# Routing one block's attention logits through DRAM, and retiming a selector group and the last staged stores, in a four-layer transformer kernel

## The chip, the cores and the metric

The kernel runs on one core of a Trainium2 chip. The metric is device time in microseconds (us). A core has a tensor engine (PE, with its weight loads PEld), a vector engine (DVE), a scalar engine (ACT), a general one (POOL) and a sync engine (SP). SP's in-order queue issues nearly all DMAs here.

## The reference

Input x is 2048 tokens of 1024 bf16 numbers. Two kinds of layer alternate, twice each, every one behind a layer norm and with a residual addition:

- Attention: x @ wqkv, 32 heads of 32. Token s looks at tokens s, s-2, ..., s-14 (8 of them). The logits are 8 dot products of length 32 per head and token; then softmax, weighted values, and @ wo.
- Gated feed-forward: relu(x @ W_gate) * (x @ W_up), 3584 wide, then @ W_down.

```
idx = pos[:, None] - arange(8) * 2
logits = einsum("bhsd,bhswd->bhsw", q, k[idx]) * 32 ** -0.5     # masked where idx < 0
o = einsum("bhsw,bhswd->bhsd", softmax(logits), v[idx]) @ wo
x = x + o;   h = relu(x @ W_gate) * (x @ W_up);   x = x + h @ W_down
```

## The kernel before

Tokens are worked in blocks of 512; a layer pair has 4 blocks, and the two pairs make blocks 0 to 7. PE does the projections and the feed-forward; DVE does the attention proper. While PE is in block n's feed-forward, DVE works on block n+1's attention. The whole program is a list of events with planned times; sorting it fixes the order on each engine. Orders are not changed at run time: a late item holds up what stands behind it in its engine's queue.

A matmul of 512 columns is a unit of 0.216 us; a group of 8 (one accumulator, "a chunk") takes GRP = 1.73 us. `acc` tiles rotate through 6 accumulators.

The logits: DVE multiplies q and k and sums over 8 chunks into s (128 partitions x 8 offsets x 512 tokens). Each head's sum is still spread over 4 partitions. It is finished in one of two ways:

```
def head_mm(n):                 # blocks 0 and 1: a "selector group" of 8 short matmuls on PE, into tile L
    for wh in range(2):         # two halves: offsets 0 to 3, then 4 to 7
        for tq in range(TPB):
            mm(st["L"][32*tq:32*tq+32, WH*wh:WH*(wh+1), :], lhsT=sel[:],
               rhs=st["s"][:, WH*wh:WH*(wh+1), tq*P:(tq+1)*P], ...)

def store_s(n): sp_dma(s_d[n % 2][:], att[n]["s"][:]...)   # other blocks: 1 MB to DRAM,
def load_s(n):  ...   # read back in 4 DMAs of 256 KB so that a head's 4 partial sums lie on one partition,
def head_sum(n):      # and added on DVE:
    dv(nc.vector.tensor_tensor, u[:], s4[:, 0:2], s4[:, 2:4], op=ALU.add)
    dv(nc.vector.tensor_tensor, u[:, 0], u[:, 0], u[:, 1], op=ALU.add)

def shift(): Lt = st["L"][:] if n < 2 else head_sum(n)
```

In the first 190 us q and k of blocks 1 to 3 go to DRAM through a pool of 6 staging tiles (`qst`, `kst`). When the first feed-forward starts, that memory is handed to its hidden tiles (r, hT), so the first relu waits for the last staged store to land:

```
pool["stage"] = ...                        # 6 staging tiles
ev.append((t_gu0 - 0.01, start_hidden))    # closes "stage", opens "hid"
spread(puts[ahead:], t_fill + GRP + 1.2, GRP)         # the last staged stores; the very last at t_gu0 + 1.2
# weight slabs (1 MB each, a ring of 5): the next one is issued 0.3 us after the end of an old slab's use
events.append((ends[i - RING] + 0.3 if i >= RING else 0.1 * i, f))
```

`[cut: layer norms, projections, weighted values (pv), output store and load (o_d, oT), output projection (wo), down projection]`

## Time and profile before

| | before |
|---|---|
| time, median of 4 runs | 1623.07 us (1621.28 to 1624.59); 1623.55 of 3 when the prediction was made |
| profiled span | 1620.6 us |
| PE busy, and its share of the chain that ended last | 99%, 93% |
| DVE busy | 70%, dense only from 40 to 370 us |
| first value matmul / last matmul starts | 9.99 / 1617.33 us |

The page's engine line (busy us, share, instructions) and its chain line (shares of the chain that ended last):

```profile
PE 1609.6 (99%) x7513; PEld 784.4 (48%) x7562; DVE 1135.1 (70%) x961; ACT 475.8 (29%) x971; POOL 174.1 (11%) x164
PE 93%; DVE 4%; DMA 1%; issue 1%; ACT 0%; SPq 0%; DVEq 0%; POOL 0%; ACTq 0%
```

99% busy does not say how much can be won. The Trainium skill ("Perfetto Trace Analysis", Identifying the Most-Contended Engine) warns that matmul busy share is a poor measure of headroom because matmuls are pipelined, and advises (Optimization Strategy) looking for the gaps on the bottleneck engine and for what ended them. This trace agrees that the share hides losses: a group of 8 is shown as 1.89 us long, but the next one starts 1.73 us after it, so a lost 0.16 us doesn't show as idle. (The page says that pipelined instructions look smaller in a trace; here they look longer, 379 ns each at starts 216 ns apart. The profiler models their ends.) The thing to read is the time from one start to the next, 0.216 us when nothing is lost. Apart from the first 10 us, PE departs from that in only three places (a distance of exactly two pitches is a matmul whose record is missing from the trace, and is passed over).

From the view of waits (engine, line, tile <- releaser: us in total, times, longest):

```profile
PE L L132 <- DVE s L106: 2.0, 2, 1.1
PE acc_g L132 <- ACT r L730: 0.2, 1, 0.2
ACT r L730 <- DMA k_d<-kst: 9.2, 1, 9.2
```

Place 1, the selector group of block 0, in the timeline (start us, duration us, engine, line, what, count, [idle before <- what ended it]):

```profile
99.17 0.40 PE L132 MATMUL L<-s,sel 128*32 128x512 bf16 x4
100.41 0.40 PE L132 MATMUL L<-s,sel 128*32 128x512 bf16 x4 [0.84 <-DVE s L106]
100.74 22.62 PE L132 MATMUL acc_v<-xnT_a,w_v 128*128 128x512 bf16 x104
```

The matmul before it started at 98.86 (99.17 less 0.31). It is 1.88 us to the next ordinary one, in place of 0.216: the second half waits for DVE to finish the second half of s. Place 2, the same in block 1:

```profile
228.88 1.89 PE L132 MATMUL acc_u<-xnT_b,w_u 128*128 128x512 bf16 x8
230.70 0.40 PE L132 MATMUL L<-s,sel 128*32 128x512 bf16 x4
232.24 0.40 PE L132 MATMUL L<-s,sel 128*32 128x512 bf16 x4 [1.14 <-DVE s L106]
232.57 1.90 PE L132 MATMUL acc_g<-xnT_b,w_g 128*128 128x512 bf16 x8
```

Here it is 2.18 us from the last `acc_u` start (230.39) to the `acc_g` at 232.57. Place 3 begins on SP. Its last k store is issued behind two weight slabs, and ACT's first relu needs that store's landing (the third line from the end is from the chain of waits in order of time: start, us, what):

```profile
191.83 0.39 SPq L121 DMA_DIRECT2D w_u<-in_B_W_up_dram  x1
192.46 0.46 SPq L121 DMA_DIRECT2D w_g<-in_B_W_gate_dram  x1
193.12 2.93 SPq L121 DMA_DIRECT2D k_d<-kst  x1
193.12 9.00 DMA k_d<-kst
202.34 1.57 ACT L730 ACTIVATE r<-acc_g 128x512 bf16<-128x512 f32 x3 [9.25 <-DMA k_d<-kst]
202.99 1.89 PE L132 MATMUL acc_g<-xnT_b,w_g 128*128 128x512 bf16 x8 [0.20 <-ACT r L730]
```

The slabs landed at 198.98 and 201.81 us, the 128 KB store at 202.12. Relu stood still for 9.25 us; PE could fill its six accumulators meanwhile (6 x 1.73 = 10.4 us) and lost only 0.36 us (0.58 between starts instead of 0.22).

### The profile page before, as it was taken

How to read it: one execution, taken by the hardware profiler on the slowest of the kernel's cores; microseconds unless marked ns; L12 is line 12 of the kernel's file. 1: busy time of each engine (PE TensorE's matmuls, PEld its weight loads, DVE VectorE, ACT ScalarE, POOL GpSimd, SP SyncE). 2: the span in 40 equal slices, each digit the busy share in tenths (PEclk: the TensorE clock that was granted, in tenths of full speed). 3: DMA queues.
4: the chain of work that ended last, by engine and by line, in shares of the span. 5: the costliest groups of instructions: out<-in, count | busy, mean ns of one | idle time of the engine just before them, and what ended most of it. 6: DMA issues, size and time to landing. Idle time of an engine off the chain costs nothing.

```text
span 1620.6 us, 18710 instructions
## 1 busy us (share of the span) xinstructions
PE 1609.6 (99%) x7513; PEld 784.4 (48%) x7562; DVE 1135.1 (70%) x961; ACT 475.8 (29%) x971; POOL 174.1 (11%) x164
## 2 busy tenths in 40 slices
PE   9999999999999999999999999999999999999999
PEld 6646544444444445444454444544445444444444
DVE  6999899995979699929479294892939939311211
ACT  4853221042116223613136031360313311131110
POOL 2300100010002002300053000530005100000000
PEclk9999999999999999999999999999999999999999
DMA  9868855689569857794757948479574884655452
GB/s 296 182 191 245 211 175 188 196 198 251 166 195 202 204 181 234 182 231 153 223 176 189 240 156 224 159 205 245 173 227 154 206 246 156 208 162 176 156 166 68
DMA packets 402695, 315.82 MB, mean 195 GB/s; under 512 B 162096, under 2 KB 384688, under 8 KB 400944
## 3 DMA queue, kind: packets, MB, share of 16 engines
q1 hardware_dynamic: 402032, 314.03, 68.4%
q8 instruction: 59, 0.97, 0.3%
q10 hardware_dynamic: 576, 0.59, 0.1%
q14 instruction: 28, 0.23, 0.0%
HBM read 265.24 MB, written 33.61 MB: 184 GB/s over the span
## 4 chain that ended last, share of the span: by engine, by line
PE 93%; DVE 4%; DMA 1%; issue 1%; ACT 0%; SPq 0%; DVEq 0%; POOL 0%; ACTq 0%
PE acc_g L132 23%; PE acc_u L132 23%; PE dacc L132 18%; PE acc_wo L132 7%; PE acc_k L132 6%; PE acc_q L132 6%; PE acc_v L132 6%; PE dacc_pair L132 6%; DVE ac L106 2%; DVE t L106 2%; DMA k_d<-kst 1%; DMA w_v<-in_A_wqkv_dram 0%; DVE s L106 0%; DVE hT L106 0%; ACT xn_a L263 0%
## 5 line engine op out<-in xcount | busy, mean ns | idle before, releaser
L132 PE MATMUL acc_g<-xnT_b,w_g 128*128 128x512 bf16 x1792 | 423.4, 379 | 0.2 <-ACT r L730 0.2
L132 PE MATMUL acc_u<-xnT_b,w_u 128*128 128x512 bf16 x1792 | 423.4, 379 | 0.0
L730 ACT ACTIVATE r<-acc_g 128x512 bf16<-128x512 f32 x224 | 133.4, 596 | 725.4 <-PE acc_g L132 660.5
L106 DVE TENSOR_TENSOR hT<-acc_u,r 128x512 bf16<-128x512 f32 x224 | 151.2, 690 | 238.2 <-PE acc_u L132 234.1
L132 PE MATMUL dacc<-w_d,hT 128*128 128x512 bf16 (+1 forms) x1372 | 300.4, 375 | 1.5
L132 PEld LDWEIGHTS <-hT 128*128 128x128 bf16 x1820 | 178.0, 98 | 209.0
L132 PEld LDWEIGHTS <-w_g 128*128 128x128 bf16 x1792 | 175.3, 98 | 211.7 <-issue 0.7
L132 PEld LDWEIGHTS <-w_u 128*128 128x128 bf16 x1792 | 175.3, 98 | 211.5
L106 DVE TENSOR_TENSOR pv<-a,vhm 128x4096 bf16<-128x4096 bf16 x64 | 143.7, 2290 | 0.0
L549 DVE TENSOR_TENSOR t<-q,k 128x2048 f32<-128x2048 bf16 x56 | 128.1, 2293 | 6.7 <-ACT k L485 4.6
L777 DVE TENSOR_TENSOR x<-dacc,x 128x512 bf16<-128x512 f32 (+1 forms) x38 | 24.5, 673 | 154.1 <-PE dacc L132 154.1
L106 DVE TENSOR_TENSOR t<-q,k 128x2048 f32<-128x2048 bf16 x56 | 127.6, 2289 | 4.0 <-ACT k L485 2.4
L106 DVE TENSOR_TENSOR pv<-pv 128x1024 bf16<-128x1024 bf16 (+1 forms) x128 | 113.9, 956 | 0.0
L132 PE MATMUL acc_wo<-w_o,oT 128*128 128x512 bf16 x498 | 111.1, 379 | 0.7
L562 DVE TENSOR_TENSOR ac<-ac,t 128x2048 f32<-128x2048 f32 x48 | 109.7, 2286 | 0.3
L106 DVE TENSOR_TENSOR ac<-ac,t 128x2048 f32<-128x2048 f32 x48 | 109.8, 2287 | 0.0
L490 POOL COPY kh<-k 128x14 bf16<-128x14 bf16 x40 | 53.7, 1347 | 511.0 <-ACT k L485 511.0
L249 POOL TENSOR_TENSOR st_b<-st_b,neg_half 128x1 f32<-128x1 f32 x29 | 40.2, 1394 | 609.7 <-ACT st_b L248 609.7
L132 PE MATMUL dacc_pair<-w_d,hT 128*128 128x512 bf16 x413 | 95.5, 379 | 0.4
L132 PEld LDWEIGHTS <-oT 128*128 128x128 bf16 x512 | 50.1, 98 | 60.3
L244 ACT ACTIVATE xn_b<-x 128x1024 bf16<-128x1024 bf16 x29 | 30.3, 1045 | 125.0 <-DVE x L703 62.1
L410 ACT CAST vT<-acc_v 128x512 bf16<-128x512 f32 x56 | 32.6, 585 | 54.8 <-PE acc_v L132 54.8
(131 smaller groups left out, 1225.2 us busy)
## 6 DMA issues: line engine op xcount, KB each, us to landing
w_g<-in_B_W_gate_dram SPq DMA_DIRECT2D x56, 1024.0 KB, 6.9
w_u<-in_B_W_up_dram SPq DMA_DIRECT2D x56, 1024.0 KB, 5.2
w_d<-in_B_W_down_dram SPq DMA_DIRECT2D x48, 1024.0 KB, 6.0
w_o<-in_A_wo_dram SPq DMA_DIRECT2D x16, 1024.0 KB, 7.1
vhm<-v_d SPq DMA_DIRECT2D x32, 284.0 KB, 6.8
v_d<-vT SPq DMA_DIRECT2D x8, 1024.0 KB, 9.3
oT<-o_d SPq DMA_DIRECT2D x32, 256.0 KB, 4.1
w_d<-in_B_W_down_dram SPq DMA_DIRECT2D x16, 512.0 KB, 3.8
```

Of the source, the lines that this page charges most:

```text
L106: tail_dve[0] = f(*args, **kwargs).ins
L132: tail_pe[0] = nc.tensor.matmul(*args, **kwargs).ins
L244: nc.scalar.activation(xn, xt[:], ACT.Square, accum_out=sq)
L249: nc.gpsimd.tensor_tensor(rstd, vpe, neg_half[:, 0:1], op=ALU.pow)
L410: tail_act[0] = nc.scalar.copy(st["vT"][:, c, :], acc[:]).ins
L490: nc.gpsimd.tensor_copy(khalo[n][:, c, :], k[:, BLK:BLK + HALO])
L549: nc.vector.tensor_tensor(t[:], i0, i1, op=ALU.mult)
L562: nc.vector.tensor_tensor(o, ac[:], t[:], op=ALU.add)
L730: tail_act[0] = nc.scalar.activation(rs[j][:], acc[:], ACT.Relu).ins
L777: run = dv if n < NB - 2 else (lambda f, *args, **kwargs: f(*args, **kwargs))
```

## The change

Its intent: take block 1's selector group off PE, remove block 0's wait, and get the last staged store ahead of the slabs. For the first of these, block 1's logits go through DRAM as the later blocks' do; the sums are stored by halves, so that the first half is away before the second is computed. Everything behind is given new times. The core of it:

```
-            sp_dma(s_d[n % 2][:], att[n]["s"][:].rearrange("p w t -> p (w t)"))
+            ws = slice(WH * half, WH * (half + 1))
+            sp_dma(s_d[n % 2][:, ws, :], att[n]["s"][:, ws, :])
...
-            Lt = st["L"][:] if n < 2 else head_sum(n)
+            Lt = st["L"][:] if n == 0 else head_sum(n)
...
-    ev.append((t_v2 + 2.2 * GRP, lambda: head_mm(0)))         # block 0's group a chunk later
-    spread(softmax_steps(0), t_v2 + 2.3 * GRP, 0.01)
+    ev.append((t_v2 + 3.2 * GRP, lambda: head_mm(0)))
+    spread(softmax_steps(0), t_v2 + 3.3 * GRP, 0.01)
...
-    spread(puts[ahead:], t_fill + GRP + 1.2, GRP)             # last staged store before the slabs
+    ev.extend((min(t_fill + GRP * (i + 1) + 1.2, t_gu0 + 0.2), f) for i, f in enumerate(puts[ahead:]))
...
-    spread(sums1[4:6], t_wo0 + 1.0, 2.5)
+    spread(sums1[4:6], t_wo0 + 0.5, 2.5)
...
-    t_head1 = t_gu0 + 37.0
-    ev.append((t_head1, lambda: head_mm(1)))
-    spread(softmax_steps(1), t_head1 + 0.1, 3.5)
...
         if n == 0:
-            spread(pv_steps(1), t_head1 + 11.5, 5.5)
-            ev.append((at + 102.0, store_o(1)))
-            ev.append((at + 102.1, load_o(1)))
+            ev.append((at + 4.0, store_s(1, 0)))
+            ev.append((at + 37.5, store_s(1, 1)))
+            ev.append((at + 40.5, load_s(1)))
             spread(gets2, at + 36.0, 2.5)
-            spread(prod_sum_steps(2), t_head1 + 11.5 + 44.5, 5.0)
+            spread(softmax_steps(1), at + 52.0, 3.6)
+            spread(pv_steps(1), at + 63.0, 5.3)
+            ev.append((at + 88.0, store_o(1, 0, 4)))
+            ev.append((at + 106.0, store_o(1, 4, 8)))
+            ev.append((at + 106.1, load_o(1)))
+            spread(prod_sum_steps(2), at + 106.0, 4.9)
...          # blocks 2 and 3: sums and outputs by halves too, times moved a few us; blocks 4 to 7: sums by halves
```

More of the change, by code (lines that the diff above doesn't have):

```diff
@@ L161 @@
     k_d = dram.tile([KC, P, S], BF16, name="k_d")
-    s_d = [dram.tile([P, W * BLK], BF16, name=f"s_d{i}") for i in range(2)]
+    s_d = [dram.tile([P, W, BLK], BF16, name=f"s_d{i}") for i in range(2)]
     zpad = const.tile([P, KC, HALO], BF16, name="zpad")
@@ L564, in prod_sum_steps, with store_s @@
         return [mult(h, c) for h in range(2) for c in range(KC)]
-    def store_s(n):
+    def store_s(n, half):
         def f():
-            sp_dma(s_d[n % 2][:], att[n]["s"][:].rearrange("p w t -> p (w t)"))
+            ws = slice(WH * half, WH * (half + 1))
+            sp_dma(s_d[n % 2][:, ws, :], att[n]["s"][:, ws, :])
         return f
@@ L924 @@
         if n == 0:
-            spread(pv_steps(1), t_head1 + 11.5, 5.5)
-            ev.append((at + 102.0, store_o(1)))
-            ev.append((at + 102.1, load_o(1)))
+            ev.append((at + 4.0, store_s(1, 0)))
+            ev.append((at + 37.5, store_s(1, 1)))
+            ev.append((at + 40.5, load_s(1)))
             spread(gets2, at + 36.0, 2.5)
-            spread(prod_sum_steps(2), t_head1 + 11.5 + 44.5, 5.0)
-        elif n + 1 < NN:
-            t_s = at + (29.0 if n < NB - 1 else 0.4)
-            ev.append((t_s - (6.0 if n < NB - 1 else 3.5), store_s(n + 1)))
-            ev.append((t_s, load_s(n + 1)))
-            spread(softmax_steps(n + 1), t_s + 13.6, 3.6)
-            spread(pv_steps(n + 1), t_s + 24.6, 6.0)
-            ev.append((t_s + 79.6, store_o(n + 1)))
-            ev.append((t_s + 79.7, load_o(n + 1)))
-            if n == 1:
-                spread(gets3, at + 24.0, 2.5)
-                spread(prod_sum_steps(3), t_s + 76.0, 4.9)
+            spread(softmax_steps(1), at + 52.0, 3.6)
[4 more added lines that the diff above has]
+            spread(prod_sum_steps(2), at + 106.0, 4.9)
+        elif n + 1 < NB:
+            ev.append((at - 8.0, store_s(n + 1, 0)))
+            ev.append((at + 28.5, store_s(n + 1, 1)))
+            ev.append((at + 32.0, load_s(n + 1)))
+            if n == 1:
+                spread(gets3, at + 46.0, 2.5)
+                spread(prod_sum_steps(3), at + 103.0, 4.9)
+            spread(softmax_steps(n + 1), at + 45.0, 3.6)
+            spread(pv_steps(n + 1), at + 56.0, 5.5)
+            ev.append((at + 79.0, store_o(n + 1, 0, 4)))
+            ev.append((at + 102.0, store_o(n + 1, 4, 8)))
+            ev.append((at + 102.1, load_o(n + 1)))
+        elif n + 1 < NN:
+            ev.append((at - 3.2, store_s(n + 1, 0)))
+            ev.append((at - 3.1, store_s(n + 1, 1)))
+            ev.append((at + 0.4, load_s(n + 1)))
+            spread(softmax_steps(n + 1), at + 14.0, 3.6)
+            spread(pv_steps(n + 1), at + 25.0, 6.0)
+            ev.append((at + 80.0, store_o(n + 1)))
+            ev.append((at + 80.1, load_o(n + 1)))
         if NB <= n + 2 < NN:
```

## The prediction

> **What bounds it now.** The tensor engine. The page gives PE 1609.6 us of a 1620.6 us span (99%) and PE 93% of the chain that ended last; granted clock 1.0. DVE is 70% busy, dense only from 40 to 370 us. Matmuls of 512 columns start 0.216 us apart. The PE timeline has only three wider gaps after the first 10 us; from 233 us to the last matmul at 1617.3 us there is none. The Trainium skill ("Perfetto Trace Analysis", Identifying the Most-Contended Engine) calls matmul busy share a poor measure, so I use starts. Only these can be won:
> 1. Selector group of block 0: its second half waits 0.84 us for DVE's s. From the value matmul before it to the next (100.74) takes 1.86 us; without a wait about 0.96 (0.31 + 0.33 + 0.32).
> 2. Selector group of block 1: a wait of 1.14 us; 2.16 us from the up matmul before it to the gate matmul after it (232.57).
> 3. At 202.99 PE waits for a gate buffer (0.58 between starts, not 0.22). ACT's relu stood 9.25 us behind the last staged k store, issued at 193.12 and landed at 202.12 behind two 1 MB slabs (issued 191.83 and 192.46, landed 198.98 and 201.81).
>
> **What the change does.**
> - Block 0's group a chunk (1.73 us) later: the wait goes, the group stays: −0.9 us.
> - Block 1 without the group: −1.94 us of PE. DVE pays two additions (2.29 + 1.22 us, as block 2 pays), DMA 1 MB out and back.
> - Last k store ahead of the slabs: lands near 195, relu follows its accumulator: PE −0.36 us, DVE −1.6 us idle there.
> - A product/sum step 0.5 us earlier fills some 3 us of DVE idle at the first output projection; half stores and earlier loads of o are off the critical path.
>
> **What could be lost.** Block 1's softmax starts 10 us later, so its outputs are complete near 298 instead of 286. The 1 MB store went only at 291.9 and landed at 301.0; now half goes early, the rest near 298. With a half store (estimate 3 to 5 us, from 1 MB in 9) and the loads (301.0 to 307.6), they are there near 308; the output projection starts near 312: slack 4 us, before 8. Loading s (1.65 us per quarter in block 2) delays an up slab, needed near 246, estimated there at 244. I expect no stall, or under 1 us.
>
> Sum −3.2 us, plus 0.2 for small waits: 1623.55 − 3.0 = about 1620.5 us, range 1619.0 to 1622.7 (8 in 10). Faster by over 2%: 0.5%; within 2%: 98.5%; slower: 1%.
>
> **What would show it.** The tile view of L keeps only block 0's 8 matmuls, no wait on DVE; no 9 us wait of relu for the k store, nor that store in the chain; no PE start gap over 0.216 us from 110 to 1617 us; DVE u goes from 12 full-width additions to 14.
>
> **What would make it wrong.** PE waiting for the up slab near 246 or the o loads near 312 us; the in-order SP queue holding slabs while it waits for s; DVE, in its fixed order, holding gate products while it waits for the loaded s until six accumulators fill (10 us); block 0's softmax, 0.9 us later, holding up its output projection (6 us slack).

## The result, and the profile after

| | before | after |
|---|---|---|
| median | 1623.07 us (4 runs, 1621.28 to 1624.59) | 1619.33 us (4 runs, 1619.23 to 1619.66) |
| profiled span | 1620.6 us | 1617.5 us |
| first value matmul to the start of the last matmul | 1607.33 us | 1603.98 us |
| start of the last matmul to the end of the span | 3.23 us | 3.70 us |

The ratio is 0.9978 (95% interval 0.9960 to 0.9995), so within 2%. Ratios are the mean time of one kernel's fast runs over that of the other's in the same rounds, so not quite the ratio of the medians quoted. The page of after, the lines that answer to those of before:

```profile
PE 1608.1 (99%) x7505; PEld 784.1 (48%) x7554; DVE 1138.3 (70%) x963; ACT 475.8 (29%) x971; POOL 176.1 (11%) x164
PE 99%; DMA 0%; issue 0%; SPq 0%; DVE 0%; DVEq 0%
```

PE's busy time is nearly the same; what changed is its share of the chain, from 93% to 99%: before, the chain ran through DVE's sums and the k store, and now it runs on PE from 10 us to the end. The timeline at the first place:

```profile
100.21 0.59 PE L132 MATMUL acc_v<-xnT_a,w_v 128*128 128x512 bf16 x2
100.74 0.62 PE L132 MATMUL L<-s,sel 128*32 128x512 bf16 x8
101.29 0.39 PE L132 MATMUL acc_v<-xnT_a,w_v 128*128 128x512 bf16 x1
```

All 8 selector matmuls stand together without a wait: from the ordinary matmul start at 100.43 to the one at 101.29 is 0.86 us instead of 1.88. At the second place nothing is left but groups 1.73 us apart:

```profile
229.07 1.89 PE L132 MATMUL acc_g<-xnT_b,w_g 128*128 128x512 bf16 x8
230.80 1.89 PE L132 MATMUL acc_u<-xnT_b,w_u 128*128 128x512 bf16 x8
```

And the third, on SP, ACT and PE:

```profile
191.94 0.32 SPq L121 DMA_DIRECT2D k_d<-kst  x1
192.36 0.39 SPq L121 DMA_DIRECT2D w_u<-in_B_W_up_dram  x1
192.84 0.59 SPq L121 DMA_DIRECT2D w_g<-in_B_W_gate_dram  x1
193.93 0.60 ACT L731 ACTIVATE r<-acc_g 128x512 bf16<-128x512 f32 x1 [2.02 <-DMA k_d<-kst]
199.72 1.89 PE L132 MATMUL acc_u<-xnT_b,w_u 128*128 128x512 bf16 x8
201.44 1.89 PE L132 MATMUL acc_g<-xnT_b,w_g 128*128 128x512 bf16 x8
```

The store landed at 193.71 us, 1.77 us after its issue instead of 9.00. That agrees with the Trainium skill ("DMA: Bandwidth & Descriptors", Queues, rings and completion order): on each DMA engine the descriptors of a queue are consumed in ring order, so a small transfer issued behind 2 MB has to wait its turn. The page adds that completion need not follow the order of issue; in this stretch the landings did.

The places gave 1.88 - 0.86 = 1.02, 2.18 - 0.22 = 1.96 and 0.36 us, 3.35 us before rounding. The distance from first to last matmul shrank by 1607.33 - 1603.98 = 3.35 us, so the three places are all of it. (The prediction's 1.86 and 2.16 leave out 0.02 us each between the starts within the selector groups.) The span changed in two other places. The first value matmul started at 9.83 instead of 9.99 (over all profiles it lay between 9.41 and 10.27, whatever the kernel). And the program's end took 0.47 us longer, which nobody had asked for; the experiments return to it.

### The profile page after: what moved, and what is told of

It is laid out like the page before. It is cut to its first block, busy times and chain, and to the rows that moved or that the text cites. A ratio compares the mean times of both kernels' runs of the same rounds, so it can differ in the third digit from the quotient of the medians.

```text
span 1617.5 us, 18722 instructions
## 1 busy us (share of the span) xinstructions
PE 1608.1 (99%) x7505; PEld 784.1 (48%) x7554; DVE 1138.3 (70%) x963; ACT 475.8 (29%) x971; POOL 176.1 (11%) x164
## 4 chain that ended last, share of the span: by engine, by line
PE 99%; DMA 0%; issue 0%; SPq 0%; DVE 0%; DVEq 0%
PE acc_u L132 24%; PE acc_g L132 24%; PE dacc L132 18%; PE acc_v L132 7%; PE acc_q L132 7%; PE acc_k L132 7%; PE acc_wo L132 7%; PE dacc_pair L132 6%; DMA w_v<-in_A_wqkv_dram 0%; PE tp L358 0%; SPq L121 0%; PE L L132 0%; DVE x L778 0%; SPq L118 0%; DVEq L1017 0%
## 5 line engine op out<-in xcount | busy, mean ns | idle before, releaser
L249 POOL TENSOR_TENSOR st_b<-st_b,neg_half 128x1 f32<-128x1 f32 x29 | 43.8, 1517 | 609.9 <-ACT st_b L248 609.9
```

The source lines that it names most:

```text
L249: nc.gpsimd.tensor_tensor(rstd, vpe, neg_half[:, 0:1], op=ALU.pow)
```

## The experiments

Theory A: each of the three PE gaps counts by itself, and nothing else in the change does. Theory B: the gain comes from DVE's work being done earlier (idle time filled, halves stored early, outputs stored early), or from the DRAM route as such. All runs gave correct results. The column "PE" is the first value matmul to the start of the last matmul, in the profiled execution; it leaves out the start-up, which differs between runs, and the end. (Two starts near 27 us were also late in e4, e10 and e12, by 0.09, 0.13 and 0.14 us in all; no edit touches that place.) "Spread" is longest minus shortest run. The medians of before in the rounds of the three groups were 1622.30, 1622.40 and 1622.49 us (9 runs each).

| run | PE us | end us | median us | runs, spread us |
|---|---|---|---|---|
| before | 1607.33 | 3.23 | 1623.07 | 4, 3.3 |
| after | 1603.98 | 3.70 | 1619.33 | 4, 0.4 |
| e1 group 0 later | 1605.90 | 3.22 | 1621.70 | 5, 1.3 |
| e2 last store early | 1605.65 | 3.22 | 1620.51 | 5, 0.4 |
| e3 group 1 later | 1606.75 | 3.22 | 1621.09 | 5, 1.6 |
| e4 the three retimed | 1604.71 | 3.21 | 1619.30 | 5, 0.5 |
| e5 after, store back | 1604.34 | 3.70 | 1619.38 | 5, 1.9 |
| e6 softmax 1 8 us later | 1604.26 | 3.71 | 1619.35 | 4, 0.8 |
| e7 whole stores | 1603.98 | 3.22 | 1618.63 | 5, 0.8 |
| e8 block 0 through DRAM | 1631.50 | 3.43 | 1645.40 | 4, 1.6 |
| e9 after again | 1603.97 | 3.70 | 1619.24 | 5, 0.8 |
| e10 late blocks whole | 1604.11 | 3.67 | 1619.34 | 5, 0.8 |
| e11 8 us later, o whole | 1606.13 | 3.81 | 1621.47 | 4, 0.7 |
| e12 whole again | 1604.12 | 3.22 | 1618.54 | 5, 0.3 |

### e1: block 0's group a chunk later, alone

```
 before
-    ev.append((t_v2 + 2.2 * GRP, lambda: head_mm(0)))     +    ev.append((t_v2 + 3.2 * GRP, lambda: head_mm(0)))
-    spread(softmax_steps(0), t_v2 + 2.3 * GRP, 0.01)      +    spread(softmax_steps(0), t_v2 + 3.3 * GRP, 0.01)
```

> The kernel before, with only block 0's selector group and softmax one chunk (1.73 us) later. Theory A (each wait of PE counts by itself): the 0.84 us wait on s goes, the last matmul starts 0.9 to 1.0 us earlier than in before (1617.3 us), time -1.0 us; the waits at 203 and 232 us stay as they are (0.36 and 1.94 us over the usual pitch). Theory B (the gain is DVE work done earlier: the idle time filled at the output projection, stores by halves, outputs stored earlier): no gain, or +0.9 since block 0's softmax is later.

PE needed 1.43 us less. The group's place went from 1.88 to 0.86 us, as theory A says. A further 0.36 came by chance: in this execution the k store landed 8.58 us after its issue instead of 9.00 (at 200.96 us), and there was no gap at 203 us. The last 0.05 us were a shorter wait at block 1's group. By time alone (0.9996, interval 0.9984 to 1.0009) the run is undecided; the chance gap is as large as the effect, which is why the trace has to decide.

### e2: the last staged store early, alone

```
 before
-    spread(puts[ahead:], t_fill + GRP + 1.2, GRP)
+    ev.extend((min(t_fill + GRP * (i + 1) + 1.2, t_gu0 + 0.2), f) for i, f in enumerate(puts[ahead:]))
```

> The kernel before, with only the last staged k store ahead of the gate slabs. Theory A: the store lands near 195 instead of 202 us, relu's 9 us wait goes, the PE gap at 203 us (0.36 us over the pitch) goes. DVE loses 1.6 us of idle there, so s of block 1 is ready 1.6 us earlier and the selector group's wait of 1.14 us shrinks to nothing too: together -1.4 to -1.5 us. Without that knock-on: -0.36 us. Theory B: about -0.4 or nothing.

The timeline of this run at block 1's selector group:

```profile
230.27 0.61 PE L132 MATMUL L<-s,sel 128*32 128x512 bf16 x8
230.81 1.47 PE L132 MATMUL acc_g<-xnT_b,w_g 128*128 128x512 bf16 x6
```

The knock-on is there: PE saved 1.68 us, 0.36 at 203 us and 1.32 at a selector group that this edit didn't touch. The late store had held back relu, relu had held back DVE's gate products, and those had held back the sums in DVE's fixed order. In before, DVE stood still for relu:

```profile
202.97 1.29 DVE L106 TENSOR_TENSOR hT<-acc_u,r 128x512 bf16<-128x512 f32 x2 [1.61 <-ACT r L730]
```

In e2 the same two products start at 201.20 us without idle time before them, the second half of s is done at 230.41 instead of 232.19 us, and PE, which comes to it at 230.49, just misses a wait. Half of the gain of the whole change (1.68 of 3.35) can be had by this one line. The five runs also lie within 0.4 us, while those of before in the same rounds lie within 1.7.

### e3: block 1's group later, staying on PE

```
 before
-    t_head1 = t_gu0 + 37.0
+    t_head1 = t_gu0 + 40.5
```

> The kernel before, with only block 1's selector group, softmax, outputs and the sums after them 3.5 us (one pair of chunks) later; the group stays on PE and nothing goes through DRAM. Theory A: the wait of 1.14 us goes, the group itself stays (0.6 to 0.75 us over the pitch): -1.2 to -1.3 us. If the DRAM trip itself is what matters (Theory B), no gain.

The group's place shrank from 2.18 to 0.86 us (-1.32), as theory A says. Yet PE saved only 0.58 us in this execution, since the gap at the k store was longer: relu waited longer, and PE with it.

```profile
ACT r L730 <- DMA k_d<-kst: 10.0, 1, 10.0
203.87 0.81 PE L132 MATMUL acc_g<-xnT_b,w_g 128*128 128x512 bf16 x3 [0.94 <-ACT r L730]
```

(The first line is from the view of waits, the second from the timeline.) The store landed at 202.99 here, and the gap was 1.32 us between starts instead of 0.58: 0.74 of the 1.32 saved was lost again. The three kernels profiled so far with the late store paid 0.36, 0 and 1.10 us at the same place.

### e4: the three retimings together, no DRAM for block 1

This is e1, e2 and e3 in one kernel.

> The kernel before with the three retimings together and no block 1 logits through DRAM, no halves. Theory A: PE gaps 1.0 + 0.36 + 1.3 gone, -2.6 to -2.8 us; that is the change (-3.5 us in PE starts) less the 0.65 us of block 1's group. Theory B: well short of it, under half of -3.5.

PE saved 2.62 us. The three places gave 1.02 + 0.36 + 1.32 = 2.70; 0.09 was lost at the two late starts near 27 us. Theory B falls: without the DRAM route, without halves and without early stores of outputs, 2.62 of the 3.35 us are there. Against after, 1604.71 - 1603.98 = 0.73 us are missing. What the DRAM route adds is 0.64 of it: the group itself, whose place had still cost 0.86 - 0.216 = 0.64 us. The rest is the 0.09 at 27 us.

```profile
232.30 0.61 PE L132 MATMUL L<-s,sel 128*32 128x512 bf16 x8
232.85 1.47 PE L132 MATMUL acc_g<-xnT_b,w_g 128*128 128x512 bf16 x6
```

The median, 1619.30, equals that of after, 1619.33. The spans of the two profiled executions show how: the 0.73 us went into an end that is 0.49 us shorter here (3.21 against 3.70) and a start-up that was 0.39 us shorter by chance (first value matmul at 9.44 against 9.83).

### e5: the change with the store put back

```
 after
-    ev.extend((min(t_fill + GRP * (i + 1) + 1.2, t_gu0 + 0.2), f) for i, f in enumerate(puts[ahead:]))
+    spread(puts[ahead:], t_fill + GRP + 1.2, GRP)
```

> The kernel after, with only the last staged k store put back behind the two slabs. Theory A (each PE gap counts by itself): the gap near 202 us returns, 0.4 to 1.1 us over the pitch (it was 0.36, 0 and 1.1 in the three profiles so far of kernels with the late store), nothing else on PE; time +0.4 to +1 us over the kernel after (1619.3), and the spread of its five runs over 1 us, where the kernels with the early store so far spread by under 0.5 us. Theory B (the k store was needed only for the selector group's wait behind it): no change, as block 1's group is gone.

```profile
201.60 1.67 PE L132 MATMUL acc_g<-xnT_b,w_g 128*128 128x512 bf16 x7 [0.19 <-ACT r L731]
```

The gap is back with 0.36 us over the pitch, and PE took exactly that much longer (1604.34 against 1603.98). The median hardly moved (1619.38), but the mean did, 1619.77 against 1619.38 of after, and the spread grew from 0.4 (0.8 in e9) to 1.9 us. Over all runs the kernels with the late store spread by 1.3 to 3.3 us, those with the early one by 0.3 to 0.8 (e8 apart, with 1.6). In the four profiles with the late store it landed 8.58, 8.99, 9.00 and 9.70 us after its issue (e1, e5, before, e3), and PE lost 0, 0.36, 0.36 and 1.10 us: beyond about 8.6 us, what the store takes longer PE loses. So the late store costs little on average and makes the time uncertain. That it also made the slowest executions slow is not shown, since one execution of each kernel was profiled.

### e6 and e11: how much slack had block 1's outputs?

e6 moves block 1's softmax and all that follows it by 8 us; e11 does the same and stores the outputs in one piece.

```
 after, both: softmax_steps(1) at + 60.0, pv_steps(1) at + 71.0, load_o(1) at + 114.1, prod_sum_steps(2) at + 114.0
 e6:  store_o(1, 0, 4) at + 96.0, store_o(1, 4, 8) at + 114.0        e11: store_o(1) at + 114.0
```

> The kernel after, with block 1's softmax, weighted values, output stores and loads and block 2's sums 8 us later. Slack theory: in after the last output load landed at 308.7 us and the first output projection started at 312.1, 3.4 us of slack; 8 us later makes PE wait 8 - 3.4 = 4.6 us there: time +4 to +6 us over the kernel after, one PE gap before the output projection of block 1. If the DVE work is farther from the critical path than that, under +1 us.

It came otherwise: PE lost 0.27 us, not 4.6. The outputs return in four DMAs, one per 128 tokens, and the output projection takes 3.45 us for each 128 tokens. It needs the first quarter to start, not the last. In after the quarters landed at 304.82, 306.43, 307.63 and 308.69 us and PE came at 311.95: the slack is 7.1 us from the first quarter, where the prediction and this expectation had taken 3 to 4 us from the last. In e6 the first quarter landed at 312.00 us, which is 7.2 and not 8 us later, and the projection started at 312.05.

> The kernel after, with block 1's softmax and all after it 8 us later, and its outputs stored in one piece. With 8 us alone the first quarter of the outputs landed at 312.0 us and PE waited only 0.27 us. If the slack counts from the first quarter's landing (304.8 in after, against PE at 312.1: 7.3 us), a whole store of 1 MB lands 1.5 to 4 us after the half did, and PE waits 1.5 to 4 us before block 1's output projection: time +1.5 to +4 us over after. If the output projection is bound by something else, under +0.5.

```profile
314.41 3.84 PE L132 MATMUL acc_wo<-w_o,oT 128*128 128x512 bf16 x17 [1.97 <-DMA oT<-o_d]
```

Here the first quarter landed at 314.4 us, PE waited for it, and lost 2.14 us there (2.35 between starts); PE's total rose by 2.15 us, and the median by 2.23 us over after in the same rounds (e9). So this slack is real and counts from the first quarter.

### e7, e10, e9 and e12: halves or whole

e7 stores every block's sums in one piece, at the time of the second half; e12 is the same kernel again. e10 keeps halves for blocks 1 to 3 and stores blocks 4 to 7 whole. e9 is the change as it stands.

```
 after, e7 and e12
-            ev.append((at + 4.0, store_s(1, 0)))
-            ev.append((at + 37.5, store_s(1, 1)))
+            ev.append((at + 37.5, store_s(1)))          # and so for the other blocks; e10: only in blocks 4 to 7
```

> The kernel after, with the sums stored whole in every block instead of by halves. Theory A: no PE gap comes of it: the loaded logits of block 1 land near 243.5 instead of 240.9 us, their first use on DVE stands at 243.8; time within 0.3 us of the kernel after. Theory B (stores by halves carry part of the gain): slower by 1 us or more.

The PE column is the same to 0.01 us. The whole store of block 1 landed at 233.39 instead of 232.10 us and the loaded logits at 242.48 instead of 240.90; DVE uses them at 243.98 and 243.76 us (e7's first value matmul is 0.22 us later). So halves of the sums carry none of the gain. The outputs were still stored by halves here; e4 stores them whole and keeps the gain too, but whole outputs alone in after were not tried. The time was lower by 0.7 us, of which 0.48 us is visible as a shorter end of the program.

> The kernel after, with the sums of blocks 4 to 7 (second layer pair) stored whole again, those of blocks 1 to 3 by halves. PE gaps as in after (none). Theory T1 (the longer end comes of the late blocks' extra stores): the end after the last matmul's start is 3.22 us as in all kernels with whole stores, time -0.5 us against after. Theory T2 (it depends on where the program's length puts the end of the sequencer's instructions): 3.2 or 3.7 or another value, not tied to the late stores.

The end took 3.67 us. T1 falls: the late blocks' extra stores are not the cause. In all profiled kernels the last output landed 2.37 to 2.43 us after the last matmul's start; only what SP does after that differs. With 836 to 844 SP records in the trace the end is 3.21 to 3.23 us, with 849 it is 3.67, with 851 3.81, with 853 3.70 to 3.71, and with 860 3.43. In after, SP's last wait before the final barrier comes 0.37 us after the one before it, with no semaphore update that late, where the same step takes 0.25 us in before (and there an output's landing explains it). T2 allowed any value, so this is no test of it: that the end depends on the program's length stays a guess, and no mechanism was found.

> The kernel after, unchanged, on the same chip and in the same rounds as the version with whole stores. Expected as before: no PE gap over the pitch between 102 and 1613 us, 3.70 us from the start of the last matmul to the end of the span, about 1619.3 us.

> The kernel after with whole stores everywhere, again, beside after in the same rounds. PE gaps none, the end 3.22 us: 0.5 us (the end) under the kernel after, about 1618.7 us; if the earlier 0.7 us was the chip's, no difference.

In the same rounds on the same chip, after took 1619.24 and the version with whole stores 1618.54 us (means 1619.32 and 1618.61). 0.48 of the 0.7 us is the end; the rest is not resolved. This is the fastest version, ahead of both kernels, by 0.04% over the change.

### e8: block 0 through DRAM too

```
 after
-            Lt = st["L"][:] if n == 0 else head_sum(n)
+            Lt = head_sum(n)
-    ev.append((t_v2 + 3.2 * GRP, lambda: head_mm(0)))
+    ev.append((t_qk0 + 45.0, store_s(0, 0)))
+    ev.append((t_v2 + 3.2 * GRP, store_s(0, 1)))
+    ev.append((t_v2 + 3.21 * GRP, load_s(0)))           # later times left as they were
```

> The kernel after, with block 0's logits through DRAM too: no selector matmul is left. PE saves the group's 0.65 us, but s is ready only at 100.4 us and DVE has nothing else to do until its logits are back (estimate 10 to 12 us, from 11.9 us between the end of s and the landing of the logits in block 1), while block 0's outputs have 6 to 7 us of slack before their output projection near 160 us: PE waits some 4 to 6 us there, perhaps again for the normalised rows near 191 us. Time +4 to +9 us over the kernel after. If DVE finds other work in that time: -0.6 us.

It cost 26 us, far more than expected. From the views of waits, and from SP's and PE's timelines:

```profile
DVE u L106 <- DMA s<-s_d: 17.7, 4, 16.1
DVE ssum L106 <- ACT d L607: 13.8, 8, 10.1
SPq L121 <- DVE ohm L106: 66.0, 13, 29.4
116.64 0.38 SPq L121 DMA_DIRECT2D w_qk_k<-in_A_wqkv_dram  x1
146.49 0.32 SPq L121 DMA_DIRECT2D o_d<-ohm  x1
157.27 3.57 PE L132 MATMUL acc_q<-xnT_a,w_qk_q 128*128 128x512 bf16 x8 [14.94 <-ACT qst L480]
163.55 5.34 PE L132 MATMUL acc_q<-xnT_a,w_qk_q 128*128 128x512 bf16 x24 [2.71 <-ACT qst L480]
186.49 4.02 PE L132 MATMUL acc_wo<-w_o,oT 128*128 128x512 bf16 x9 [5.51 <-DMA w_o<-in_A_wo_dram]
```

The expectation counted DVE's wait and the outputs' slack. It left out SP's queue. DVE waited 16.1 us for the logits and 10.1 for the exponential, which stood on ACT behind six q evictions. SP, in order, had the first output store next and stood still from 117 to 146.5 us; behind it stood the q stores that free the staging tiles; all six were full, ACT could evict nothing, and PE stopped for 15 us in the middle of the q projection, well before the output projection. PE's clock then fell, as the windows view shows (window: us, then busy us of each engine and count, granted clock, DMA share, GB/s):

```profile
140.00:157.00 17.00, 2.33 (x11) 1.44 (x10) 17.00 (x17) 0.37 (x1) 0.00 (x0) 0.63 0.52 159
157.00:164.00 7.00, 4.02 (x11) 1.59 (x11) 7.00 (x9) 1.30 (x4) 0.00 (x0) 0.68 1.05 273
```

The granted clock, third number from the end, is 0.63 and 0.68 on average in these windows. The Trainium skill ("TensorE: Matmul & The Clock Gate", Part 1) states that PE falls to half its clock after an idle window of about 3.4 us and comes back after about as long a busy one. This trace agrees on the half: the matmuls after the stop start up to 0.43 us apart, twice 0.216. The times are only of that order: the half clock lasts from 144.5 to 161.5 and from 185.4 to 192.2 us, so it begins 2.2 and 4.4 us after the end of the last matmul and is over 4.2 and 5.7 us after the next one starts. The three stops add 15.1 + 3.1 + 5.7 = 23.9 us over the pitch. The 21 starts at the slower clock add 4.3 us. Together that is 28.2 us: the 27.5 us that PE lost and the 0.64 us that the missing group saved. Whether block 0's route could pay with all later times moved along was not tried; what is to be had there is the 0.64 us of its group.

## Why the prediction was right, and where it was not

The prediction, 1620.5 us in a range of 1619.0 to 1622.7, held: 1619.33 us. That the number lies inside the range is partly luck: it contains 0.47 us at the program's end that nobody foresaw. e7 and e12, which do the same on PE with the old end, took 1618.63 and 1618.54 us, below the range. The mechanism held better than the number.

- What bounds the kernel. Right. PE alone, and in three places only; the change removed exactly those, and from 102 us to the last matmul no start came later than the pitch.
- Block 0's group: -0.9 predicted, -1.02 measured. The term left for the group without a wait, 0.96 us, was 0.86: its two halves run closer together than the estimate said. e1 shows the step alone.
- Block 1's group: -1.94 predicted, -1.96 measured. But the reason "without the group" is a small part of it: e2 and e3 show that 1.32 of it is the wait, which a retiming, or the early k store alone, removes. The DRAM route as such is worth 0.64 us (e4).
- The k store: -0.36 predicted and measured. Right for the kernel as a whole. The prediction did not say that this step alone also removes block 1's wait (e2), nor that the store's landing differs from execution to execution and with it PE's gap, from 0 to 1.1 us.
- No new stall. Right; DVE's additions for the loaded logits went from 12 to 14 as announced, and in block 1 it used its logits at 243.8 us without waiting (they landed at 240.90), the up slab landed at 244.15 (estimated 244), the outputs were complete at 297 us (298), and the projection started at 311.95 (312).
- The slack of the outputs, "4 us, before 8". Wrong in size: it was counted from the last quarter's landing; PE needs the first. It is 7.1 us, as e6 and e11 show. The error was on the safe side.
- Half stores "off the critical path". Right for PE as to the sums (e7), so these were not worth making: the version without them is 0.7 us faster, mainly at the program's end, which the prediction did not look at. Half stores of the outputs bring them in earlier (e6 against e11), which counts only once the slack is used up.
- The 1.2 us between forecast and result are mostly not the mechanism's. 0.15 us is in the terms above (3.35 against 3.2) and 0.2 was put on for waits that did not come; the longer end works the other way. The rest was not taken apart. The likely place is a reference that scatters: the median of before was 1623.55 when the prediction was made, 1623.07 with a fourth run, and 1622.30 to 1622.49 in the later rounds. Against those, after's second set of runs is 1622.49 - 1619.24 = 3.25 us faster.

## What to carry to other kernels

When an engine is 99% busy, look through the starts of its instructions for those later than the usual pitch: the list was short here, and it gave the gain before the first run. Then ask of each wait whether moving the waiting instruction a chunk later would do; here that and one DMA issued ahead of two large ones gave 2.7 of 3.35 us, and the new data route only 0.64. In an in-order DMA queue, put a small store that frees memory ahead of large prefetches, and when a producer becomes later, move every queue entry that waits for it along with it.

## What the Trainium skill lacked or had wrong

- "TensorE: Matmul & The Clock Gate", Back-to-back issue gap, gives about 131 ns per matmul of 512 columns in a sustained stream of weight loads and matmuls, and about 216 ns only for the isolated case. Here the sustained stream with a weight load before every matmul ran at 216 ns, at full granted clock, over 1600 us. (An earlier section of the page, on the phases of a matmul, does give 216 ns as the back-to-back gap.)
- The same page, Part 3 (packing small matmuls), has no figure for the cost of putting a packed group between ordinary matmuls. Here 8 selector matmuls of 32 output partitions made the distance between the ordinary ones 0.86 us instead of 0.216, of which about 0.31 us passed before the first and 0.31 after the last.
- "DMA: Bandwidth & Descriptors" explains ring order, but shows no case of what it does to a small transfer: a 128 KB store took 1.77 us when it was issued ahead of two 1 MB loads, and 9.00 us behind them.
- No page that I read mentions that the end of a program can vary from kernel to kernel: here 3.21 to 3.81 us from the last matmul's start, with the last output always landing after 2.37 to 2.43 us. The cause is open.
